# Two of the first loads of an attention and MLP kernel move to another queue, constants go first, and three dummy matmuls are added

## The chip, the cores and the metric

The kernel runs as one program on one core of a Trainium2 chip. The core has five engines with their own instruction streams: TensorE (PE in the rows, with PEld for its weight loads), VectorE (DVE), ScalarE (ACT), GpSimd (POOL) and SyncE (SP). They wait for each other by semaphores. Transfers between main memory and the on-chip buffers are issued by an engine, here almost always SP, and carried out by 16 DMA engines. The metric is the device time of the whole program in microseconds (us); lower is better. The runs shown are medians of three, and one further execution was recorded by the hardware profiler.

## What is computed

The reference takes q, k, v of shape (2, 8, 768, 64), batch, heads, sequence and head size, and runs three stages one after the other:

```python
# 1. linear attention with a decay per head
for t in range(S):
    state = gamma * state + einsum('bhd,bhe->bhde', k[:, :, t], v[:, :, t])
    y[:, :, t] = scale * einsum('bhd,bhde->bhe', q[:, :, t], state)
x = y.transpose(0, 2, 1, 3).reshape(B, S, H * D)            # (2, 768, 512)
# 2. channel mixing with the token before
xk = mu_k * x + (1 - mu_k) * x_prev;  xr = mu_r * x + (1 - mu_r) * x_prev
x = sigmoid(xr @ w_r) * (maximum(xk @ w_k, 0) ** 2 @ w_v)
# 3. gated MLP with a mixing over the sequence
u, v = split(gelu(x @ w_in));  v_n = normalise(v) * g_ln
out = x + (u * (w_sg @ v_n + b_sg)) @ w_out
```

The first stage is the one that the change touches. Of the weights and of q, k and v all bytes come from main memory; the weights arrive as 64-bit floats and are turned into pairs of 32-bit numbers on ACT and DVE.

## The kernel before

The attention is done in chunks of 128 steps, 6 chunks of the sequence times 2 batches, so 12 chunks that are numbered 0 to 11 with the batch changing fastest. Chunk i has two loads of 512 KB each: `qk` (q and k with the feature along the partitions) and `kv` (k and v with the step along the partitions), both issued by `loads` (line 353). For each chunk PE computes

- the scores, key by query, 8 matmuls for the 8 heads (`scores`, line 412, tile `sc`, rows with L416); DVE multiplies them by a mask (`decay`, line 420, tile `prs`, L425),
- the state that the chunk adds, from the keys and the scaled values (`state`, L452, tile `st`); the scaled values `vs` are made on DVE for chunks 0 and 1 (L434) and on POOL for the rest (L430),
- the output from the state of the chunks before (`inter`, L478, tile `y`), which needs a copy of `st` into `scr` that ACT or DVE makes (L249), for all but chunks 0 and 1,
- the output within the chunk (`intra`, L489, tile `y`), from `prs` and `vs`.

In the trace each of these matmuls shows as two, so a chunk's scores are x16. DVE then writes the tokens into `x` (L503), and prepares operands `mix` and `xo` for the second stage, whose matmuls (L327, `kp`, `rp`, `vp`) follow without a break, while the eight pieces of `w_k` are loaded (L256) and converted (L275 to L298).

Before the first scores PE runs ten dummy matmuls of 512 columns on a tile of zeros (`warm_mm`, line 393). `const` (line 363) loads a small table with the mask and the decays, `scratch` (line 374) a table for the outputs.

The order of the instructions on every engine is not written out: each piece of work is handed to a `Plan` (line 54) with an engine, a cost in us, what it reads and writes and the buffers that it takes, and `Plan.order` (line 88) replays these costs and sets the order, and with "DVE ACT" also the engine. Loads go through a model of the transfers there: an issue keeps SP for `ISSUE`, data follow `DMA_LEAD` later at `DMA_RATE`, all in one line (`link`). So a change of a cost or of a queue can move work of all engines. When the program runs, the engines wait only for what they need: data, buffers, and one of eight slots for transfers from the hardware queues, which are used in turn.

Of the kernel before, what the change touches and what calls it, by code (L numbers as in the profile page):

```python
# [33 lines left out]
RSQRT_SEED = float(0x5F3759DF)  # L34
PIECE = 512
WARM_UP = 10
EARLY = 5
CHUNKS = 8
XO = 4
# [8 lines left out]
ISSUE = 0.4  # L48
ADD_ISSUE = 1.2
DMA_LEAD = 1.4  # L50
DMA_TAIL = 2.0
DMA_RATE = 0.41
# [6 lines left out]
class Plan:  # L59
# [28 lines left out]
    def order(self):  # L88
        ops, n = self.ops, len(self.ops)
        left = [len(o[3]) for o in ops]  # L90
        after = [[] for _ in ops]
# [10 lines left out]
                wait.setdefault(pool, []).append((i, kind))  # L102
        home = {}
        pending = {}
        engines = ("PE", "DVE", "ACT", "POOL", "SP", "ADD")
        idle = {e: BEGIN for e in engines}
        queue = {e: [] for e in engines}
        seq, events, link = [], [(BEGIN, -1, e) for e in engines], 0.0
        started = [False] * n

        def put(i):
# [26 lines left out]
            return True  # L138

        def start(i, t, eng):  # L140
            nonlocal link
            engs, cost, fn, deps, new = ops[i]
            engs = engs.split()
            if len(engs) > 1:
                cost = cost[engs.index(eng)]
            for e in engs:
                queue[e].remove(i)
            on[i] = eng
            started[i] = True
            for pool, kind, buf, make in new:  # L150
                free[pool] -= 1
                held[pool, kind] = held.get((pool, kind), 0) + 1
                home[buf] = (pool, kind)
                wait[pool].remove((i, kind))
            if eng in ("SP", "ADD"):
                busy = t + (ISSUE if eng == "SP" else ADD_ISSUE)
                late = link > t + DMA_LEAD + 1.0
                link = max(t + DMA_LEAD, link) + cost / DMA_RATE
                done = link + (DMA_TAIL if late else 0.8)
            else:  # L160
                busy = done = t + cost
            idle[eng] = busy
            seq.append(i)
            heapq.heappush(events, (done, i, "near"))
            heapq.heappush(events, (done + LINK, i, "far"))
            heapq.heappush(events, (busy, n, eng))
# [5 lines left out]
        while events:  # L172
            t = events[0][0]
            while events and events[0][0] <= t + 1e-9:
                _, i, eng = heapq.heappop(events)
# [29 lines left out]
def fused_kernel(ctx, tc, qk, kv, w_k, w_v, w_r, w_in, w_sg, w_out, consts, ydec, b_sg, out):  # L205
# [32 lines left out]
    def new_b(kind, buf):  # L238
        return new("ps", kind, buf, (128, 512))
# [113 lines left out]
    def loads(i, what):  # L353
        b, c = chunks[i]
        hold = [(("kv", 0), 0)] if i > 1 else []
        if "q" in what:
            plan.op("SP", .525, lambda: sp.dma_start(out=T["qk", i], in_=qk[b, c]), r=hold, w=[(("qk", i), 0)],
                    new=[new_p("chunk", ("qk", i), (128, 2, KD, CH), F32)])
        if "v" in what:
            plan.op("SP", .525, lambda: sp.dma_start(out=T["kv", i], in_=kv[b, c]), r=hold, w=[(("kv", i), 0)],  # L360
                    new=[new_p("chunk", ("kv", i), (128, 2, H, D), F32)])

    def const():
# [25 lines left out]
        w = T["warm"] = pools["t"].tile([128, 512], BF16, tag="t", name="warm")  # L389
        dve.memset(w, 0.0)  # L390

    def warm_mm():
        for _ in range(WARM_UP):
            pe.matmul(out=T["warmps"], lhsT=T["warm"][:, :128], rhs=T["warm"], start=True, stop=True)

    prs_new = ("bA", "prs", "prs", products)
    scr_new = ("bB", "scr", "scr", lambda: None)
    plan.op("DVE", .3, warm, w=[("warm", 0)], new=[("t", "warm", "warm", lambda: None)])
    plan.op("PE", 4.0, warm_mm, r=[("warm", 0)], w=[("warmps", 0)], new=[new_b("warm", "warmps")])
    loads(0, "q")  # L400
    plan.op("SP", .11, const, w=[("con", 0)])
    loads(0, "v")
    loads(1, "qv")
    plan.op("SP", .26, scratch, r=[(("kv", 0), 0)], w=[("scr", "yd")], new=[scr_new])
# [89 lines left out]
    def tokens(c):  # L494
        n, off = divmod(c * CH, BW)
        x = ("x", n)
        if off == 0 and n == 0:
            plan.op("DVE", .1, lambda: dve.memset(T[x][:, :, :, 0:1], 0.0), w=[(x, "p")],
                    new=[new("x", "x", x, (128, KD, B, BW + 1))])
        for e in range(2):  # L500
            def scale(e=e):
                table = T["yt", c % 2] if c else T["yd"]
                dve.tensor_tensor(out=T[x][:, e::2, :, 1 + off:1 + off + CH],  # L503
                                  in0=T["y", c, e].rearrange("p (b j t) -> p j b t", b=B, t=CH),
                                  in1=table[:, e::2].unsqueeze(2).to_broadcast([128, KD // 2, B, CH]), op=ALU.mult)
            plan.op("DVE", .66, scale, r=[(("y", c, e), 0), ("scr", ("yt", c % 2) if c else "yd")], w=[(x, (e, off))],
                    new=[new("x", "x", x, (128, KD, B, BW + 1))] if off == 0 and e == 0 and n else [])
        if off == 0 and n:
            plan.op("DVE", .15, lambda: dve.tensor_copy(T[x][:, :, :, 0:1], T["x", n - 1][:, :, :, BW:BW + 1]),
                    r=[(("x", n - 1), (e, CH)) for e in range(2)], w=[(x, "p")])  # L510

    for c in range(NCH):
        pair = (B * c, B * c + 1)
        for i in pair:
            if i > 1:
                loads(i, "qv")
        for step in (scores, decay, inter, state, intra):
            for i in pair:
                step(i)
        tokens(c)  # L520

    def prep(n, kk, i):
# [492 lines left out]
```

## Time and profile before

| | us |
|---|---|
| median of 3 runs (lowest, highest) | 357.09 (356.94, 358.16) |
| the profiled execution | 359.38 |
| its span, from first to last instruction | 357.60 |
| PE busy in it | 347.6 (97%) |
| DVE, ACT, POOL busy | 255.8 (72%), 159.7 (45%), 28.8 (8%) |
| granted TensorE clock, mean | 1.00 |

The span is shorter than the execution's own time by 1.78 us that lie around it. PE's share is so high that the few stretches in which it is not busy are where the time is decided, and these lie in the first 45 us and in the last 12. Over the first 40 us the transfers fill the 16 DMA engines: in the page's 40 slices of 8.9 us the first four carry 252, 415, 408 and 409 GB/s, later ones rarely over 200. The constants are 106 KB, the output table 256 KB, every chunk load and every piece of `w_k` 512 KB.

A row of the timeline gives start and length of a group of equal instructions, then engine, line, operation, tiles and count, and in brackets how long the engine stood idle before it and what ended that.

### The profile page before, as it was taken

How to read it: one execution, taken by the hardware profiler on the slowest of the kernel's cores; microseconds unless marked ns; L12 is line 12 of the kernel's file. 1: busy time of each engine (PE TensorE's matmuls, PEld its weight loads, DVE VectorE, ACT ScalarE, POOL GpSimd, SP SyncE). 2: the span in 40 equal slices, each digit the busy share in tenths (PEclk: the TensorE clock that was granted, in tenths of full speed). 3: DMA queues.
4: the chain of work that ended last, by engine and by line, in shares of the span. 5: the costliest groups of instructions: out<-in, count | busy, mean ns of one | idle time of the engine just before them, and what ended most of it. 6: DMA issues, size and time to landing. Idle time of an engine off the chain costs nothing.

```text
span 357.6 us, 5412 instructions
## 1 busy us (share of the span) xinstructions
PE 347.6 (97%) x2130; PEld 289.7 (81%) x2130; DVE 255.8 (72%) x501; ACT 159.7 (45%) x274; POOL 28.8 (8%) x29
## 2 busy tenths in 40 slices
PE   7988999999999999999999999999999999999995
PEld 4777788888888888888888888888888888899884
DVE  1778999898992664568699998999995656535431
ACT  1044669888972543345589659734542000000000
POOL 0453400000002122101100000000000000000000
PEclk9999999999999999999999999999999999999999
DMA  7999555135544669406354245121130000110122
GB/s 252 415 408 409 210 185 170 59 92 161 158 141 98 106 183 168 73 3 173 66 172 119 60 122 173 44 79 55 45 88 2 0 0 0 60 59 2 58 90 89
DMA packets 15689, 43.32 MB, mean 121 GB/s; under 512 B 1456, under 2 KB 3632, under 8 KB 15664
## 3 DMA queue, kind: packets, MB, share of 16 engines
q1 hardware_dynamic: 12944, 37.73, 30.9%
q0 software_dynamic: 2720, 5.24, 8.6%
q8 instruction: 17, 0.28, 0.3%
q14 instruction: 8, 0.07, 0.1%
HBM read 32.48 MB, written 3.15 MB: 100 GB/s over the span
## 4 chain that ended last, share of the span: by engine, by line
PE 88%; DMA 7%; DVE 3%; issue 1%; SPq 0%; ACT 0%; DVEq 0%; ACTq 0%
PE vp L327 26%; PE kp L327 18%; PE sp L327 14%; PE up L327 9%; PE rp L327 9%; PE op L327 7%; DMA chunk<-qk 3%; DMA chunk<-kv 2%; DMA out<-o 2%; PE y L489 2%; PE sc L416 1%; PE y L478 1%; DVE o L910 1%; DVE xo L316 1%; PE st L452 1%
## 5 line engine op out<-in xcount | busy, mean ns | idle before, releaser
L327 PE MATMUL kp<-xo,wk 128*128 128x512 f32 x288 | 66.2, 390 | 0.0
L327 PEld LDWEIGHTS kp<-xo,wk 128*128 128x128 f32 x288 | 53.9, 188 | 11.5 <-issue 0.3
L327 PE MATMUL sp<-wsg,vh 128*128 128x512 f32 (+1 forms) x288 | 50.2, 336 | 0.0
L327 PEld LDWEIGHTS sp<-wsg,vh 128*128 128x128 f32 x288 | 44.4, 190 | 5.7
L327 PE MATMUL vp<-k,wv 128*128 128x512 f32 x168 | 38.9, 389 | 0.0
L327 PEld LDWEIGHTS vp<-k,wv 128*128 128x128 f32 x168 | 31.5, 188 | 6.5
L327 PE MATMUL vp<-win,x2o 128*128 128x512 f32 x144 | 33.3, 389 | 0.0
L327 PE MATMUL up<-x2o,win 128*128 128x512 f32 x144 | 33.1, 389 | 0.0
L327 PE MATMUL rp<-xo,wr 128*128 128x512 f32 x144 | 33.1, 389 | 0.0
L327 PE MATMUL op<-gt,wout 128*128 128x512 f32 x144 | 33.0, 389 | 0.0
L327 PEld LDWEIGHTS rp<-xo,wr 128*128 128x128 f32 x144 | 27.0, 188 | 5.6
L327 PEld LDWEIGHTS vp<-win,x2o 128*128 128x128 f32 x144 | 27.0, 188 | 5.6
L327 PEld LDWEIGHTS up<-x2o,win 128*128 128x128 f32 x144 | 27.0, 188 | 5.6
L327 PEld LDWEIGHTS op<-gt,wout 128*128 128x128 f32 x144 | 27.0, 188 | 5.6
L888 DVE SCALAR_TENSOR_TENSOR g<-sp,con,bsg 128x512 f32<-128x512 f32 x12 | 9.0, 751 | 21.8 <-PE sp L327 21.8
L316 DVE TENSOR_TENSOR xo<-mix,xo 128x512 fp32r<-128x512 f32 x24 | 17.0, 735 | 8.9 <-ACT xo L249 8.8
L910 DVE TENSOR_TENSOR o<-op,x 128x256 f32<-128x256 f32 (+1 forms) x20 | 8.8, 474 | 19.8 <-PE op L327 13.8
L275 ACT ACTIVATE cv<-raw 128x512 f32<-128x512 f32 x32 | 21.5, 670 | 1.9 <-DMA raw<-w_in 0.7
L327 PE MATMUL vp<-k,ws 128*128 128x512 f32 x96 | 22.1, 389 | 0.0
L612 POOL DMA_DIRECT2D raw<-wv x10 | 12.1, 1211 | 116.9 <-DMA raw<-wv 86.4
L327 PEld LDWEIGHTS vp<-k,ws 128*128 128x128 f32 x96 | 18.0, 188 | 3.7
L290 DVE SCALAR_TENSOR_TENSOR cv<-cv,raw 128x512 int32<-128x512 int32 x28 | 19.8, 714 | 0.6 <-ACT raw L283 0.6
(104 smaller groups left out, 464.5 us busy)
## 6 DMA issues: line engine op xcount, KB each, us to landing
chunk<-qk SPq DMA_DIRECT2D x12, 512.0 KB, 10.1
chunk<-kv SPq DMA_DIRECT2D x12, 512.0 KB, 10.1
raw<-wv POOLq DMA_DIRECT2D x10, 512.0 KB, 5.1
raw<-w_k SPq DMA_DIRECT2D x8, 512.0 KB, 5.3
raw<-w_v SPq DMA_DIRECT2D x8, 512.0 KB, 3.6
raw<-w_in SPq DMA_DIRECT2D x8, 512.0 KB, 3.5
out<-o SPq DMA_DIRECT2D x12, 256.0 KB, 2.2
raw<-w_sg SPq DMA_DIRECT2D x6, 384.0 KB, 3.2
```

Of the source, the lines that this page charges most:

```text
L275: plan.op("ACT", .68, lambda: act.activation(out=xf(), in_=word(1).bitcast(F32), func=ACTF.Prelu, scale=-F64_REBIAS * F64_SIGN, alpha=1.0 ...
L290: dve.scalar_tensor_tensor(out=xi(), in0=xi(), scalar=3, in1=word(0), op0=ALU.logical_shift_left, op1=ALU.bitwise_or)
L316: plan.op("DVE", .69, lambda: dve.tensor_tensor(out=lo(), in0=src(), in1=hi(), op=ALU.subtract), r=[*keep, (buf, ("hi", part))], w=[(buf, ...
L327: pe.matmul(out=T[ps][:, cols], lhsT=l(), rhs=r(), start=first and q == 0 and i == 0, stop=q == 2 and i == len(grp) - 1, skip_group_check= ...
L416: pe.matmul(out=T["sc", i, p][:, j * CH:(j + 1) * CH], lhsT=a[par[p], 1, j], rhs=a[par[p], 0, j], start=j == 0, stop=j == KD - 1, skip_gro ...
L452: pe.matmul(out=st[par[p], b, j], lhsT=T["kv", i][:, 0, h], rhs=T["vs", i][:, h], start=c == 0 and b == 0 and j == 0, stop=b == B - 1 and ...
L478: pe.matmul(out=y_at(i, j, p), lhsT=T["sbd", (c - 1) % 2][par[p], b, j], rhs=T["qk", i][par[p], 0, j], start=b == 0 and j < 2, stop=False, ...
L489: pe.matmul(out=y_at(i, j, p), lhsT=T["vs", i][:, 2 * j + p], rhs=T["pr", i % 4][:, p, j], start=c == 0 and b == 0 and j < 2, stop=b == B ...
L612: plan.op("ADD", .53, lambda t=t: pool.dma_start(out=T[raw], in_=block_view(*t), accum_op=ALU.add), r=[(b, ("hi" if not t[2] else "lo", p) ...
L888: dve.scalar_tensor_tensor(out=out_, in0=in_, scalar=T["vec"][:, 2, m:m + 1], in1=t.unsqueeze(1).to_broadcast([128, B, BW]) if last else t ...
L910: plan.op("DVE", .69 if g == B else .42, lambda n=n, ps=ps, o=o, m=m, part=part, of=of: dve.tensor_tensor(out=T[o][:, part], in0=T[ps][:, ...
```

## The change

The loads of `kv` for chunks 0 and 1 are issued by ACT instead of SP. The constants are issued before the first chunk. Three dummy matmuls are put behind the scores of chunk 0. In the planner's model ACT gets a line of transfers of its own ("AQ"), which runs at half rate, as does SP's until 7.5 us; the ten dummies cost 4.3 instead of 4.0.

```diff
--- before.py
+++ after.py
@@ -34,6 +34,8 @@
 RSQRT_SEED = float(0x5F3759DF)
 PIECE = 512
 WARM_UP = 10
+FILL = 3
+SHARED = 7.5
 EARLY = 5
 CHUNKS = 8
 XO = 4
@@ -102,10 +104,11 @@
                 wait.setdefault(pool, []).append((i, kind))
         home = {}
         pending = {}
-        engines = ("PE", "DVE", "ACT", "POOL", "SP", "ADD")
+        engines = ("PE", "DVE", "ACT", "POOL", "SP", "ADD", "AQ")
         idle = {e: BEGIN for e in engines}
         queue = {e: [] for e in engines}
         seq, events, link = [], [(BEGIN, -1, e) for e in engines], 0.0
+        link2 = 0.0
         started = [False] * n
 
         def put(i):
@@ -138,7 +141,7 @@
             return True
 
         def start(i, t, eng):
-            nonlocal link
+            nonlocal link, link2
             engs, cost, fn, deps, new = ops[i]
             engs = engs.split()
             if len(engs) > 1:
@@ -152,11 +155,15 @@
                 held[pool, kind] = held.get((pool, kind), 0) + 1
                 home[buf] = (pool, kind)
                 wait[pool].remove((i, kind))
-            if eng in ("SP", "ADD"):
-                busy = t + (ISSUE if eng == "SP" else ADD_ISSUE)
-                late = link > t + DMA_LEAD + 1.0
-                link = max(t + DMA_LEAD, link) + cost / DMA_RATE
-                done = link + (DMA_TAIL if late else 0.8)
+            if eng in ("SP", "ADD", "AQ"):
+                busy = t + (ADD_ISSUE if eng == "ADD" else ISSUE)
+                if eng == "AQ":
+                    link2 = max(t + DMA_LEAD, link2) + 2 * cost / DMA_RATE
+                    done = link2 + 0.8
+                else:
+                    late = link > t + DMA_LEAD + 1.0 and t > SHARED
+                    link = max(t + DMA_LEAD, link) + (2 if link < SHARED else 1) * cost / DMA_RATE
+                    done = link + (DMA_TAIL if late else 0.8)
             else:
                 busy = done = t + cost
             idle[eng] = busy
@@ -357,7 +364,7 @@
             plan.op("SP", .525, lambda: sp.dma_start(out=T["qk", i], in_=qk[b, c]), r=hold, w=[(("qk", i), 0)],
                     new=[new_p("chunk", ("qk", i), (128, 2, KD, CH), F32)])
         if "v" in what:
-            plan.op("SP", .525, lambda: sp.dma_start(out=T["kv", i], in_=kv[b, c]), r=hold, w=[(("kv", i), 0)],
+            plan.op("SP" if hold else "AQ", .525, lambda: (sp if hold else act).dma_start(out=T["kv", i], in_=kv[b, c]), r=hold, w=[(("kv", i), 0)],
                     new=[new_p("chunk", ("kv", i), (128, 2, H, D), F32)])
 
     def const():
@@ -389,16 +396,16 @@
         w = T["warm"] = pools["t"].tile([128, 512], BF16, tag="t", name="warm")
         dve.memset(w, 0.0)
 
-    def warm_mm():
-        for _ in range(WARM_UP):
+    def warm_mm(count):
+        for _ in range(count):
             pe.matmul(out=T["warmps"], lhsT=T["warm"][:, :128], rhs=T["warm"], start=True, stop=True)
 
     prs_new = ("bA", "prs", "prs", products)
     scr_new = ("bB", "scr", "scr", lambda: None)
     plan.op("DVE", .3, warm, w=[("warm", 0)], new=[("t", "warm", "warm", lambda: None)])
-    plan.op("PE", 4.0, warm_mm, r=[("warm", 0)], w=[("warmps", 0)], new=[new_b("warm", "warmps")])
+    plan.op("PE", 4.3, lambda: warm_mm(WARM_UP), r=[("warm", 0)], w=[("warmps", 0)], new=[new_b("warm", "warmps")])
+    plan.op("SP", .11, const, w=[("con", 0)])
     loads(0, "q")
-    plan.op("SP", .11, const, w=[("con", 0)])
     loads(0, "v")
     loads(1, "qv")
     plan.op("SP", .26, scratch, r=[(("kv", 0), 0)], w=[("scr", "yd")], new=[scr_new])
@@ -517,6 +524,9 @@
         for step in (scores, decay, inter, state, intra):
             for i in pair:
                 step(i)
+                if step is scores and i == 0:
+                    plan.op("PE", .65, lambda: warm_mm(FILL), r=[("warm", 0)], w=[("warmps", 0)],
+                            after=plan.writer[("sc", 0, 0), 0])
         tokens(c)
 
     def prep(n, kk, i):
```

What the planner makes of it, at three places. First the loads at the start of SP's stream; chunk_93, 110, 112, 114, 133 are qk 0, kv 0, qk 1, kv 1, qk 2, and scr0 takes the output table. Before:

```order
L357 DMA chunk_93<-qk 128x1024
L372 DMA con_108<-consts 128x212
L360 DMA chunk_110<-kv 128x1024
L357 DMA chunk_112<-qk 128x1024
L360 DMA chunk_114<-kv 128x1024
L381 DMA scr0_128<-ydec 128x512
L357 DMA chunk_133<-qk 128x1024
```

Now, with chunk_108, 112, 133 for qk 0, 1, 2 and chunk_135 for kv 2:

```order
L379 DMA con_93<-consts 128x212
L364 DMA chunk_108<-qk 128x1024
L364 DMA chunk_112<-qk 128x1024
L388 DMA scr0_120<-ydec 128x512
L364 DMA chunk_133<-qk 128x1024
L367 DMA chunk_135<-kv 128x1024
```

and at the start of ACT's stream, where the two loads stand ahead of the table that ACT loads for its functions (chunk_110 and 114 are kv 0 and kv 1):

```order
L1020 UNCONDITIONAL_BRANCH
L367 DMA chunk_110<-kv 128x1024
L367 DMA chunk_114<-kv 128x1024
L256 ACT_TABLE_LOAD
L256 COPY scr0_120<-st_147 128x512
```

The constants moved from second to first, and the two `kv` loads from SP, where they stood third and fifth, to ACT, where nothing stands ahead of them.

Second the start of PE's stream, from the last of the ten dummies on, to the first output from the state (L478, now L485). Before:

```order
L394 MATMUL warm<-warm 128x512
L416 MATMUL sc<-chunk 128x128 x8
L452 MATMUL st<-vs,chunk 64x64 x8
L489 MATMUL y<-prs_137,vs 64x128 x8
L416 MATMUL sc<-chunk 128x128 x16
L452 MATMUL st<-vs,chunk 64x64 x8
L489 MATMUL y<-prs_137,vs 64x128 x8
L478 MATMUL y<-chunk,scr_128 64x128 x8
```

Now (two of the three dummies left out):

```order
L401 MATMUL warm<-warm 128x512
L423 MATMUL sc<-chunk 128x128 x8
...
L401 LDWEIGHTS warm
L401 MATMUL warm<-warm 128x512
L459 MATMUL st<-vs,chunk 64x64 x8
L496 MATMUL y<-prs_142,vs 64x128 x8
L423 MATMUL sc<-chunk 128x128 x8
L459 MATMUL st<-vs,chunk 64x64 x8
L423 MATMUL sc<-chunk 128x128 x8
L496 MATMUL y<-prs_142,vs 64x128 x8
L485 MATMUL y<-chunk,scr_120 64x128 x8
```

Beside the dummies, the state of chunk 1 now comes before the scores of chunk 2, and the output of chunk 1 after them.

Third, PE from the state of chunk 2 to the output of chunk 5. Before:

```order
L452 MATMUL st<-vs,chunk 64x64 x8
L489 MATMUL y<-prs_138,vs 64x128 x8
L452 MATMUL st<-vs,chunk 64x64 x8
L489 MATMUL y<-prs_138,vs 64x128 x8
L416 MATMUL sc<-chunk 128x128 x16
L478 MATMUL y<-chunk,scr_129 64x128 x16
L452 MATMUL st<-vs,chunk 64x64 x8
L489 MATMUL y<-prs_137,vs 64x128 x8
L452 MATMUL st<-vs,chunk 64x64 x8
L489 MATMUL y<-prs_137,vs 64x128 x8
```

Now:

```order
L459 MATMUL st<-vs,chunk 64x64 x8
L496 MATMUL y<-prs_143,vs 64x128 x8
L423 MATMUL sc<-chunk 128x128 x8
L459 MATMUL st<-vs,chunk 64x64 x8
L496 MATMUL y<-prs_143,vs 64x128 x8
L485 MATMUL y<-chunk,scr_121 64x128 x8
L423 MATMUL sc<-chunk 128x128 x8
L485 MATMUL y<-chunk,scr_121 64x128 x8
L459 MATMUL st<-vs,chunk 64x64 x8
L496 MATMUL y<-prs_142,vs 64x128 x8
L459 MATMUL st<-vs,chunk 64x64 x8
L496 MATMUL y<-prs_142,vs 64x128 x8
```

The scores of chunk 4 moved ahead of the state and output of chunk 3, and those of chunk 5 behind the first output of chunk 4. Further on the scores of chunk 8 stand directly ahead of chunk 8's output from the state, where before a state and an output of chunk 7 stood between. On SP two pieces of `w_k` moved ahead of the `qk` of chunk 7, and one behind its `kv`. From the first full run of second-stage matmuls on, PE's stream is the same as before.

## Rows read from the trace of the kernel before

**Rows 1.** Stretches: busy time of each engine, then clock, DMA share, GB/s.
```profile
core 0: us, PE busy (x) PEld busy (x) DVE busy (x) ACT busy (x) POOL busy (x), PEclk, DMA share, GB/s
0.00:4.00 4.00, 2.81 (x7) 1.04 (x8) 0.29 (x2) 1.28 (x1) 0.20 (x4) 1.00 0.54 174
4.00:6.50 2.50, 2.50 (x12) 1.23 (x12) 0.17 (x1) 0.00 (x0) 0.00 (x0) 1.00 0.85 224
6.50:8.00 1.50, 1.01 (x12) 0.82 (x9) 0.33 (x1) 0.00 (x0) 0.00 (x0) 1.00 1.03 412
34.00:38.00 4.00, 2.93 (x56) 2.20 (x54) 4.00 (x6) 1.62 (x3) 2.17 (x2) 1.00 1.03 412
45.30:345.40 300.10, 300.10 (x1417) 251.40 (x1414) 221.61 (x448) 142.86 (x248) 12.11 (x10) 1.00 0.33 90
```

**Rows 2.** Chain of waits that ended last: start, length, what.
```profile
10.22 11.15 DMA chunk<-qk
...
25.66 1.91 issue
...
45.41 1.12 PE kp L327 x4
...
48.55 34.72 PE kp L327 x152
```

**Rows 3.** Timeline of PE, from the start to 35 us.
```profile
1.20 4.45 PE L394 MATMUL warm<-warm 128*128 128x512 bf16 x10 [1.20 <-DVE x L498]
5.57 1.94 PE L416 MATMUL sc<-chunk 64*128 64x128 f32 x16
8.42 0.69 PE L452 MATMUL st<-vs,chunk 128*64 128x64 f32 x16 [0.91 <-DVE vs L434]
...
10.63 1.16 PE L416 MATMUL sc<-chunk 64*128 64x128 f32 x16
...
14.87 0.67 PE L478 MATMUL y<-chunk,scr 64*64 64x128 f32 x16
...
18.54 0.63 PE L452 MATMUL st<-vs,chunk 128*64 128x64 f32 x16
...
21.51 1.16 PE L416 MATMUL sc<-chunk 64*128 64x128 f32 x16 [0.19 <-DMA chunk<-qk]
...
34.50 0.38 PE L416 MATMUL sc<-chunk 64*128 64x128 f32 x2 [0.24 <-issue]
```

**Rows 4.** Timeline of DVE, the first 11 us.
```profile
4.34 0.17 DVE L407 TENSOR_SCALAR omu<-con 128x8 f32<-128x8 f32 x1 [3.18 <-DMA con<-consts]
7.67 0.69 DVE L434 TENSOR_TENSOR vs<-chunk,con 128x512 f32<-128x512 f32 x1 [3.16 <-DMA chunk<-kv]
...
10.23 0.69 DVE L434 TENSOR_TENSOR vs<-chunk,con 128x512 f32<-128x512 f32 x1 [0.67 <-DMA chunk<-kv]
```

**Rows 5.** Timeline of SP's issues (SPq), early and later.
```profile
4.37 0.88 SPq L360 DMA_DIRECT2D chunk<-kv  x1
...
22.67 0.33 SPq L357 DMA_DIRECT2D chunk<-qk  x1
23.95 0.33 SPq L360 DMA_DIRECT2D chunk<-kv  x1
```

**Rows 6.** Timeline of POOL: scaling of chunk 4's values.
```profile
20.17 1.04 POOL L430 TENSOR_TENSOR vs<-chunk,con 128x512 f32<-128x512 f32 x1 [3.08 <-DMA chunk<-kv]
```

**Rows 7.** DMA queues from 24.9 to 26.3 us: packets, MB, share.
```profile
q8 instruction: 1, 0.02, 4.8%
```

**Rows 8.** Timeline of all engines, 34 to 38 us.
```profile
34.43 1.52 DVE L533 SCALAR_TENSOR_TENSOR mix<-x,con,mix 128x512 f32<-128x512 f32 x1
...
36.57 0.58 ACT L249 COPY scr<-st 128x512 f32<-128x512 f32 x1
...
37.20 0.67 PE L478 MATMUL y<-chunk,scr 64*64 64x128 f32 x16 [0.83 <-ACT scr L249]
```

**Rows 9.** Timeline of DVE: last low half of the first weight.
```profile
61.47 0.68 DVE L298 TENSOR_TENSOR wk<-cv,wk 128x512 fp32r<-128x512 f32 x1
```

## The prediction

> **What bounds the kernel now.** First the stretches: between 45.30 and 345.40 us TensorE (PE) is busy 300.10 of 300.10 us, and the 357.6 - 345.4 = 12.2 us after that belong to the last results and their stores [rows 1]. The matmuls there are the same ones before and after the change, in the same order, so 312 of the 357.6 us can only stay or get worse. What the change can win lies ahead of 45.3 us, in the attention stage.
>
> Second the chain of waits for that part: it is DMA until 21.37, then PE, with a hole of 1.91 us at 25.66 that nothing in the program explains [rows 2]. Third, PE's timeline and the queues beside it, for the start, where the change is.
>
> I call chunk i's loads qk i and kv i, its score, state and two output products sc i, st i, y i and, with the earlier state, x i. PE runs ten dummies from 1.20 to 5.65 at 0.43 us each, sc0 from 5.57 with no wait before it, st0 at 8.42 after a wait of 0.91 for DVE, y0, and sc1 at 10.63 [rows 3]. 512 columns in 0.43 us are the pace of 1.2 GHz; sc0 runs at it too (1.94 us against 1.16 for sc1), although the stretches print a granted clock of 1.00. VectorE (DVE) has the constants at 4.34, kv0 only at 7.67, kv1 at 10.23 [rows 4]. So the start is held by kv0, third in the queue, and not by qk0.
>
> **The start, step by step.** The same eight transfers are issued, six on SyncE (SP) and two on ScalarE (ACT). Nobody waits for an issue, and ACT, which issues two of them now, has nothing to do from 4 to 8 us [rows 1]. What delays landing is the engines that move bytes: 224 GB/s from 4.0 to 6.5 us, 412 after it [rows 1]. In the weak stretch 2.5 x (412-224)/412 = 1.14 us of transfer were lost, just when an issue took 0.88 us, where it takes 0.33 later [rows 5]. Rows do not say why. In the forecast it happens again.
>
> Constants, qk0 and kv0 are 0.106 + 0.524 + 0.524 = 1.154 MB. In the old order qk0 came first; now it shares its time with kv0, and both are in when all 1.154 MB are. By the stretches 4.0 x 174 GB/s = 0.69 MB had moved by 4.0 and the rest, 0.46 at 224 GB/s, by 6.1. Constants and first chunk (0.63 MB) had moved before 4.0 and were seen at 4.34, so I add 0.4: both are there at 6.5. Bounds: 5.6 (qk0 in its old place, no wait) and 7.7 (kv0's old place). The Trainium skill (DMA: Bandwidth & Descriptors, Issuing engines are not separate DMA queues) says the same against this change: DMAs from SP, ACT and POOL run on the same 16 engines and interleave, and a second issuer saves issue time alone. No run here shows two such queues yet; by this rule the second queue brings no byte earlier, and the working does without it.
>
> So sc0 starts at 6.5 instead of 5.57 and, at the pace of 1.94 us, ends at 8.4. The three dummies behind it cost 3 x 0.43 = 1.3 us at the low clock, half of it at the high one; no row shows which, so I take the middle, 0.95: to 9.35. Behind them wait st0 and everything else on PE. Part of that is covered, as y0 has to wait for DVE's first masking pass, about 0.7 us after sc0. st0 takes 0.6, to 9.95; kv0's scaling (0.69) is long done, which saves the wait of 0.91 before st0 [rows 3]; y0 1.05, to 11.0. qk1 and kv1 close the same sum of bytes as kv1 did, 10.23 [rows 4]. Then sc1 to 12.1, st1 (0.5) to 12.6, sc2 to 13.7 (now ahead of y1), y1 to 14.6. Before: 14.87 [rows 3]. The start gains 0.3 us, between 0.6 gained and none with the dummies' two prices.
>
> **Where that goes.** From y1 both orders do x2, sc3, x3, st2, y2: from 14.87 to 18.54 then [rows 3], 3.7 us, so now to 18.3. The new order then puts sc4 ahead of st3 and y3. kv4 lands at 20.17 [rows 6], and issues that wait for a free slot come 1.28 us apart, one load each [rows 5], so qk4 lands about 18.9: PE waits 0.6. Then sc4 1.1, st3 0.5, y3 0.9, x4 0.5, sc5 1.1 and x5 0.5 end at 23.6. Before, sc5 waited for qk5 until 21.51 [rows 3] and with it x4 and x5 were through 2.1 us later, at 23.6. So 0: the loads, whose sum and start do not change, take back whatever the start wins, and a start up to 0.6 us later than worked out here costs nothing either.
>
> The hole from 25.66 to 27.57 stands ahead of y5 and has no releaser, only "issue" [rows 2]. In the 1.4 us around it the DMA rows show one transfer of the instruction queue, 0.02 MB [rows 7]; PE seems to have run out of instructions while their fetch stood behind data. The Trainium skill (Runtime: NRT & Kernel Launch, Instruction fetch mechanics) has PE refilled in 16 KiB blocks, the cost of a boundary "mostly hidden". The trace agrees on the block and not on the hiding: 1.91 us here. By the rule the hole would be something else; the sum carries it unchanged either way. Six more PE instructions move the boundary by six. I leave the hole as it is: 0. Bounds: down to the next such hole, 0.24 at 34.50 [rows 3], so -1.7; and as much again, +1.9.
>
> **34 to 38 us.** PE is busy 2.93 of 4.00 us [rows 1]. 0.83 of the rest is x8 waiting for ACT's copy of the state, which came at 36.57, behind a cast that itself waited for a DVE pass of 1.52 us (other passes over as many elements take 0.69 [rows 4]) [rows 8]. The new order has sc8 (1.09) between y7 and x8, so PE has work while the copy is made: -0.8. Bounds 0 (the wait turns up elsewhere) and -1.07.
>
> **Weight loads, later stages.** On SP two w_k pieces are now ahead of qk7: +2 x 1.28 = 2.56 us for it. It stood five loads behind kv4 (20.17 [rows 6]), so at 26.6, and goes to 29.1; y5 ends 1.0 after the hole, at 28.6, and sc7 comes at 28.6 + 1.1 + 0.5 + 0.5 = 30.7, a cover of 1.6 us. If the hole went, some 0.3 would show. DVE and ACT share the weight conversions in another way; the last w_k piece is through at 62.2 [rows 9] and wanted by the eighth result of 12 matmuls each, of which four came at 45.41: at 48.55 + (84-4) x 34.72/152 = 66.8 [rows 2], 4.6 us of slack. In the long stretch DVE is busy 74% and ACT 48% [rows 1]: 0, at worst some tenths.
>
> **Sum.** Start and loads 0, hole 0, state copy -0.8, rest 0: -0.8. On the profiled execution 359.38 - 0.8 = 358.6. The median before is 357.09, 2.29 under that execution, so I forecast 357.09 - 0.8 = **356.3 us**.
>
> **Rivals.**
> - *The weak stretch of the transfers goes.* It coincides with slow issues in one queue, which speaks for it; that bytes first moved well with the same queue speaks against. Then every load is 1.1 us earlier, sc0 starts at 5.6, PE reaches the hole about 1.0 earlier, and if the fetch is asked for earlier too, all of it lasts: -1.0 - 0.8 = -1.8, 355.3. With the hole shrunk as well, 354.
> - *PE goes idle after the dummies and stays slow (slower).* sc0 waits for qk0 until 7.7: 2.1 us of idle PE at the low clock, sc0 to 9.65, dummies 1.3 to 10.95, st0 and y0 to 12.6, sc1, st1, sc2, y1 to 16.3: 1.4 later than before. The loads hide 0.3 of it up to the hole, but the hole's end is pushed by the full 1.4 if the fetch is asked for at PE's pace; and the state copy is then asked for at another moment, so its gain is not sure: +1.4, 358.5, or 357.7 with that gain. It decides from sc0 later than about 7. For it speaks kv0's row at 7.67, against it that 0.69 MB had moved by 4.0.
> - *Nothing is left.* The start washes out as worked above, and DVE's and POOL's collisions fall on another state copy: 357.1.
>
> **How the numbers follow.** Forecast 0.40, weak stretch gone 0.24, slow start 0.13, nothing left 0.23. 0.5% of 357.09 is 1.8 us, about what a measurement of this kernel tells from no change: under 355.3 is faster, over 358.9 slower. Half of the second case and some tenths of a shrunken hole in the first give 0.22 faster; slow starts with a grown hole give 0.09 slower; 0.69 between. The range holds the forecast with the bounds of hole and copy, most of the weak-stretch case (down to 354.6) and the slow start (358.4).
>
> **What would show it.** Right: sc0 at 6 to 7 with a gap behind the dummies, kv0 seen on DVE beside it, kv1 at about 10.2, sc4 waiting for a DMA near 18.9, a hole without releaser near y5, no ACT wait ahead of x8, and PE without idle time from about 44.5. Wrong: 400 GB/s between 4 and 6.5 us and sc5 before 20.5 (the first rival); sc0 after 7, or sc1 still at 1.9 us (the second); PE waiting for anything after 46 us, which the sum puts at nothing.

## The result, and the profile after

The changed kernel takes 359.53 us (median of 9 runs, 358.30 to 360.33) against 356.93 (9 runs, 356.69 to 358.16) of the kernel before on the same chip: ratio 1.0066, 95% interval 1.0048 to 1.0084. It is slower on this chip, above the forecast of 356.3 and above the range. Its profiled execution took 359.12 us with a span of 356.9.

The stretches after, to be laid beside [rows 1]: busy time and number of instructions of each engine, then granted clock, DMA share and GB/s.

```profile
core 0: us, PE busy (x) PEld busy (x) DVE busy (x) ACT busy (x) POOL busy (x), PEclk, DMA share, GB/s
0.00:4.00 4.00, 2.81 (x7) 1.04 (x8) 0.29 (x2) 1.28 (x1) 0.20 (x4) 1.00 0.49 126
4.00:6.50 2.50, 1.01 (x4) 0.24 (x2) 0.86 (x2) 0.00 (x0) 0.00 (x0) 1.00 1.03 421
...
8.00:12.00 4.00, 4.00 (x45) 2.67 (x44) 2.39 (x3) 0.00 (x0) 2.04 (x2) 0.62 1.03 410
...
34.00:38.00 4.00, 4.00 (x74) 3.24 (x70) 4.00 (x8) 2.99 (x5) 1.11 (x2) 1.00 1.02 402
...
45.30:345.40 300.10, 300.04 (x1413) 251.22 (x1413) 221.22 (x448) 143.90 (x248) 12.14 (x10) 1.00 0.33 90
```

One of the forecast's two signs of the first rival stands in them: between 4.0 and 6.5 us the transfers move 421 GB/s instead of 224, so the weak stretch is gone (in the 4 us ahead of it they move less, 126 instead of 174). The other sign, sc 5 before 20.5, failed: it starts at 23.23. PE is busy for only 1.01 of the 2.5 us, and from 8 to 12 us it has a granted clock of 0.62, which fits the second rival. The stretch 34 to 38 us is full, 4.00 of 4.00, where it was 2.93.

PE's timeline after, for [rows 3]: start, length, operation, in brackets the idle time ahead and what ended it.

```profile
1.19 3.81 PE L401 MATMUL warm<-warm 128*128 128x512 bf16 x10 [1.19 <-DVE x L505]
7.55 2.03 PE L423 MATMUL sc<-chunk 64*128 64x128 f32 x16 [2.55 <-DMA chunk<-qk]
9.52 1.46 PE L401 MATMUL warm<-warm 128*128 128x512 bf16 x3
10.91 0.73 PE L459 MATMUL st<-vs,chunk 128*64 128x64 f32 x16
...
12.45 1.16 PE L423 MATMUL sc<-chunk 64*128 64x128 f32 x16
...
23.23 1.16 PE L423 MATMUL sc<-chunk 64*128 64x128 f32 x16
...
44.01 1.20 PE L334 MATMUL kp<-xo,wk 128*128 128x512 f32 x4
45.14 2.73 PE L496 MATMUL y<-prs,vs 128*64 128x128 f32 x32
```

PE waits 2.55 us for qk 0, then runs sc 0 and the dummies at half its pace; st 0 starts at 10.91 instead of 8.42. So the second rival's sign "sc0 after 7" came; its other one, sc 1 at 1.9 us, did not (1.16 at 12.45). PE never waits for a load or an engine again before the long stretch. The result products of chunks 10 and 11 (y at 45.14) take 2.73 us, against 1.97 in the trace of the kernel before that follows below. DVE, for [rows 4]: the constants at 4.82, and kv 0, for which it waited until 7.67 before, at 5.14, with nobody to use it until sc 0 is done. The last two lines show why y 10 and y 11 are slow: three conversions take DVE 3.39 us (1.88 in the kernel with qk 0 first, below), and so it makes the `prs` that these products read only from 44.25 to 46.72.

```profile
4.82 0.17 DVE L414 TENSOR_SCALAR omu<-con 128x8 f32<-128x8 f32 x1 [3.67 <-DMA con<-consts]
5.14 0.69 DVE L441 TENSOR_TENSOR vs<-chunk,con 128x512 f32<-128x512 f32 x1
9.61 1.29 DVE L432 TENSOR_TENSOR prs<-sc,con 128x512 f32<-128x512 f32 x2 [3.78 <-PE sc L423]
...
39.66 3.39 DVE L297 SCALAR_TENSOR_TENSOR cv<-cv,raw 128x512 int32<-128x512 int32 x3
...
44.25 2.47 DVE L432 TENSOR_TENSOR prs<-sc,con 128x512 f32<-128x512 f32 x4
```

Why qk 0 came so late stands in the DMA queues of the changed kernel from 3 to 4 us (q10 is ACT's queue, q1 SP's; packets, MB, share of the 16 engines):

```profile
q10 hardware_dynamic: 82, 0.34, 81.5%
q1 hardware_dynamic: 77, 0.06, 18.2%
```

The two queues got nearly the same number of packets through, but SP's were those of the constants, 0.8 KB each, and ACT's those of kv 0, 4.1 KB each. While the constants stand in front of qk 0, ACT's queue takes the bytes. The Trainium skill (DMA: Bandwidth & Descriptors, Queues, rings and completion order) says that each DMA engine goes round between the queues it has work for, a packet at a time; the 82 to 77 packets agree, as far as a packet of these rows is what the page calls one. The counts are not always that close: in the kernel with qk 0 first (below) the constants pass from 4 to 5 us, and there SP's queue has 112 packets and 0.13 MB, ACT's 69 and 0.22 MB. In both stretches the queue with the small packets moves fewer bytes.

### The profile page after: what moved, and what is told of

Its sections match the earlier page's. It is cut to its first block, busy times and chain, and to the rows that moved or that the text cites. A ratio compares the mean times of both kernels' runs of the same rounds, so it can differ in the third digit from the quotient of the medians.

```text
span 356.9 us, 5411 instructions
## 1 busy us (share of the span) xinstructions
PE 348.9 (98%) x2133; PEld 289.9 (81%) x2133; DVE 256.1 (72%) x501; ACT 160.2 (45%) x274; POOL 28.8 (8%) x29
## 3 DMA queue, kind: packets, MB, share of 16 engines
q10 hardware_dynamic: 288, 1.05, 0.7%
## 4 chain that ended last, share of the span: by engine, by line
PE 83%; DMA 11%; DVE 4%; SPq 0%; issue 0%
PE vp L334 26%; PE kp L334 18%; PE sp L334 14%; PE up L334 9%; PE rp L334 9%; DMA chunk<-qk 7%; PE op L334 7%; DMA chunk<-kv 2%; DMA out<-o 2%; DVE prs L432 1%; DVE cv L297 1%; DVE o L920 1%; DVE x L510 1%; PE y L496 0%; DVE xo L323 0%
## 5 line engine op out<-in xcount | busy, mean ns | idle before, releaser
L432 DVE TENSOR_TENSOR prs<-sc,con 128x512 f32<-128x512 f32 x24 | 15.3, 681 | 7.7 <-PE sc L423 7.6
```

The source lines that it names most:

```text
L432: plan.op("DVE", .66, lambda p=p: dve.tensor_tensor(out=T["pr", i % 4][:, p], in0=heads(T["sc", i, p]), in1=T["mask"].unsqueeze(1).to_broa ...
```

## The experiments

Twelve runs were made, in four groups, each group on one chip beside the kernel before (358.04, 357.77, 357.75 and 358.58 us there). In the expectations, W says that PE's wait for qk 0 and the low clock are what costs, O that the new order does, H that the recorded execution of before was not its usual one, S that recording itself costs; further letters are explained in the expectation in which they first stand. Times are medians. Ratios are to the kernel before in the same group, with 95% intervals; they are not the quotients of the medians. Different groups ran on different chips, so medians are compared within a group. Five numbers of the profiled runs carry most of the reading: when sc 0, st 0 and the first four matmuls of the second stage (kp) start, how long y 10 and y 11 take, and the span, in us.

| profiled run | sc 0 | st 0 | kp x4 | y 10, 11 | span |
|---|---|---|---|---|---|
| before, again | 5.57 | 8.54 | 43.20 | 1.97 | 355.4 |
| changed, again | 7.07 | 10.47 | 43.87 | 2.73 | 356.7 |
| changed, no dummies behind sc 0 | 7.24 | 9.24 | 43.62 | 2.75 | 356.5 |
| new order, loads on SP | 5.04 | 8.66 | 43.05 | 2.72 | 355.9 |
| old order, kv 0 and 1 on ACT | 5.57 | 7.06 | 41.78 | 1.97 | 353.9 |
| the same, 15 dummies | 6.04 | 7.26 | 43.56 | 1.97 | 355.7 |
| changed, 18 dummies | 7.04 | 8.88 | 42.79 | 2.72 | 355.7 |
| the same, POOL writes only | 7.31 | 9.15 | 41.84 | 1.97 | 354.0 |
| changed, qk 0 before constants | 5.57 | 7.67 | 41.20 | 1.97 | 353.3 |
| the same, again | 5.15 | 7.24 | 41.04 | 1.97 | 353.2 |
| the same, no dummies behind sc 0 | 5.26 | 7.41 | 41.52 | 1.97 | 353.7 |
| constants first, qk 0 and kv 0 on ACT | 5.57 | 8.44 | 41.55 | 1.97 | 353.7 |

**The kernel before, unedited.**

> The kernel before, unchanged, recorded once more. Theory H (the recorded execution of before was not a usual one: its hole of 1.91 us ahead of y5, and its own time of 359.38 against a median of 356.93, belong together): the hole is shorter by 1.5 us or more in the new record, or stands elsewhere, and the first second-stage matmul starts at 43 to 43.8 us, not 45.34. Rival S (the record is a usual one and recording itself costs the 2.4 us): hole and 45.3 us come back within 0.3 us. The ratio is 1.000 within 0.2% by both.

357.56 us (356.39 to 359.86, 12 runs), ratio 0.9987 (0.9962 to 1.0011). Its profiled run shows no wait of PE for "issue": the hole of 1.91 us [rows 2] is not in it, nor in any later profiled run of this study. H holds for that term: the trace that the prediction rests on was one of the longer executions.

```profile
12.44 1.16 PE L416 MATMUL sc<-chunk 64*128 64x128 f32 x16 [0.53 <-DMA chunk<-qk]
...
31.80 1.16 PE L416 MATMUL sc<-chunk 64*128 64x128 f32 x16 [0.91 <-DMA chunk<-qk]
...
44.35 1.97 PE L489 MATMUL y<-prs,vs 128*64 128x128 f32 x32
```

It waits for loads, 0.53 and 0.91 us; in these two places they hold the old order.

**The changed kernel without its three dummies.**

```diff
-plan.op("PE", .65, lambda: warm_mm(FILL), ...
+plan.op("PE", .65, lambda: warm_mm(0), ...
```

> The changed kernel with its order and queues, without the three dummies behind chunk 0's scores. Theory W (PE waits for qk0 until 7.5 us, runs at the low clock until about 11, and never idles again, so whatever the start loses stays): the dummies' 1.46 us at the low clock come off in part, since the first masking pass then ends at 10.9 and holds y0: y0 at 10.9 instead of 11.5, total 0.5 to 1.5 us below the changed kernel (358.0 to 359.0). If the dummies are what brings the clock back, chunk 0's outputs run at the low pace instead and nothing is gained or 1 us lost (359.5 to 360.5). Theory O (the order of the work is what costs): no change, 359.5.

358.56 us (12 runs), ratio 0.9992 (0.9970 to 1.0013); two runs at 355.88 and 356.09 with a mean granted clock of 1.0, ten from 357.89 to 358.83 at 0.994 to 0.998. In the profiled run sc 0 still waits (to 7.24) and still takes 2.08 us; st 0 is then slow too (1.12 us). So the dummies behind sc 0 cause neither the wait nor the low pace. What they cost in time is not shown: the changed kernel did not run in this group, and the ratio shows no loss against the kernel before. The median lies in W's range and not at O's 359.5, but these came from times on another chip.

**New order and dummies, the first loads on SP as before.**

```diff
-lambda: (sp if hold else act).dma_start(out=T["kv", i], ...
+lambda: sp.dma_start(out=T["kv", i], ...
+# first five issues put back: qk0, con, kv0, qk1, kv1
```

> The changed kernel's order of work and its dummies, but the first five loads all from SP and in the sequence of before (first chunk's qk, constants, kv, qk, kv). Theory W: chunk 0's scores start at 5.6 again with no idle time behind the ten dummies, so most of the loss goes: 356.5 to 357.5, at or within 0.2% of before. Theory O: the loss stays, 359 to 360.

357.31 us, ratio 0.9966 (0.9941 to 0.9992): no loss against the kernel before. In the profiled run sc 0 starts at 5.04, and the granted clock is 1.00 up to 12 us. O falls; W stands.

**Old order, only kv 0 and kv 1 on ACT.**

```diff
-lambda: sp.dma_start(out=T["kv", i], ...
+lambda: (sp if hold else act).dma_start(out=T["kv", i], ...
```

> The kernel before, in its own order and without the extra dummies, with the kv loads of chunks 0 and 1 issued by ACT and nothing else; qk0 is first on SP. Theory W: qk0 shares with kv0 and lands about 7.0 (constants no longer ahead of it, so 0.3 before the changed kernel), the scores start at 7.0 to 7.3 at the low clock: 1 to 2 us over before, 358 to 359. Theory O: as before, 357.0, or 0.5 to 1 us faster, since the loads behind gain (400 GB/s and over from 4 to 6.5 us).

357.36 us, ratio 0.9956 (0.9934 to 0.9978), in two groups, five runs at 355.78 to 356.16 and seven at 357.3 to 357.8, six of these with a mean clock of 0.995 to 0.997. Here qk 0 is first on SP and is in by 5.57. W had expected it at 7.0 and a loss of 1 to 2 us, because it shares the engines with kv 0; that failed, and the gain of 0.7 us is within what O had named. So a second queue is no loss by itself; with qk 0 in front it is a gain.

**The changed kernel, unedited, on another chip.**

> The changed kernel unedited, beside the next three on one chip. Theory Q (the constants, issued first on SP, push the issue of qk 0 from 0.74 to 1.19 us, behind kv 0 and kv 1 that ACT's queue issues at 0.74; qk 0 then lands near 7.5, PE idles 2.5 us and runs on at half the clock until 11) and theory C (what costs is the idle of PE and the low clock after it, whatever made qk 0 late) both expect it slower than before by 0.4 to 0.9% again, near 359, with clock records under 1.0 in the first 12 us. Theory R (the loss was a matter of that chip and hour, and the start is hidden behind DVE and the loads) expects it level with before within 0.3%.

358.93 us (356.05 to 359.36, 12 runs), ratio 1.0014 (0.9990 to 1.0038). The trace repeats the late start, but three runs of 356.05 to 357.75 blur the ratio; by the ratio alone this group does not tell slower from same, and R is not ruled out by it. The mean clock does not set these three apart (0.999 and 1.0): the slowest run, 359.36, has 1.0 too.

```profile
1.19 4.45 PE L401 MATMUL warm<-warm 128*128 128x512 bf16 x10 [1.19 <-DVE x L505]
7.07 2.08 PE L423 MATMUL sc<-chunk 64*128 64x128 f32 x16 [1.43 <-DMA chunk<-qk]
```

The clock records under 1.0 that Q and C expected in the first 12 us are not there. The ten dummies took 4.45 us, 0.43 us each, which is the pace of 1.2 GHz by the prediction's working, and sc 0 went on at it behind the wait. So here the clock did not fall: PE had not left the lower level when it began to wait, and the profile prints 1.00 all the same. In the first trace the ten dummies took 3.81 us; there PE had left it, and the clock fell behind the wait. The run without the dummies behind sc 0 is like this one (4.45, then 1.59 idle).

**qk 0 ahead of the constants.** The one edit that the rest turns on: order and dummies as changed, kv 0 and kv 1 still on ACT.

```diff
+# first two SP issues swapped: qk0, con
```

> The changed kernel with one pair of issues changed back on SP: qk 0 first, constants second; kv 0 and kv 1 stay on ACT's queue, order and dummies as changed. Theory Q: qk 0 is in before 5.6 as in the run with the order of before and ACT's loads, sc 0 starts by 5.6, no clock record under 1.0 in the profile, st 0 near 7.3 instead of 10.9, kp near 42 to 42.5 instead of 44.0; 356.0 to 357.0, some 2 us under the changed kernel beside it. Theory C alone, with qk 0 late because ACT's queue is served first whatever SP's order: sc 0 still at 7, 358.5 to 359.5. Theory R: within 0.5 us of the changed kernel.

355.38 us (355.31 to 355.71, 6 runs), ratio 0.9933 (0.9909 to 0.9957): faster than both kernels, below Q's range, and with the narrowest spread of all. It is 3.55 us under the changed kernel beside it, so R falls, and C alone with it. Its queues from 3 to 4 us and its PE:

```profile
q1 hardware_dynamic: 49, 0.20, 51.2%
q10 hardware_dynamic: 49, 0.20, 48.8%
```

```profile
5.57 1.41 PE L428 MATMUL sc<-chunk 64*128 64x128 f32 x16
6.91 0.82 PE L405 MATMUL warm<-warm 128*128 128x512 bf16 x3
7.67 0.69 PE L464 MATMUL st<-vs,chunk 128*64 128x64 f32 x16
```

Now qk 0 and kv 0 do share evenly, as the forecast had assumed for the changed kernel; Q holds.

**The changed kernel with 18 first dummies.**

```diff
-plan.op("PE", 4.3, lambda: warm_mm(WARM_UP), ...
+plan.op("PE", 4.3, lambda: warm_mm(18), ...
```

> The changed kernel with 18 dummy matmuls ahead of sc 0 instead of 10 (some 0.21 us each once the clock is up, so that they end at 6.7 to 7.3 instead of 5.0 to 5.6); loads, order and the three dummies behind sc 0 as changed. qk 0 still lands at 7.5. Theory C: sc 0 at 7.5 now takes 1.2 us instead of 2.0 and the three dummies 0.65 instead of 1.46, so st 0 starts near 9.3 instead of 10.9: 1.4 to 1.6 us under the changed kernel beside it, 357.2 to 357.8, with no clock record under 1.0 in the first 12 us. Theory Q with the clock as a mere companion (the lateness of qk 0 is all): no more than 0.4 under the changed kernel. Theory R: the same as the changed kernel within 0.3.

357.36 us (355.79 to 358.28), ratio 0.9978 (0.9957 to 0.9998), 1.6 us under the changed kernel beside it.

```profile
7.04 1.16 PE L423 MATMUL sc<-chunk 64*128 64x128 f32 x16 [0.45 <-DMA chunk<-qk]
8.13 0.82 PE L401 MATMUL warm<-warm 128*128 128x512 bf16 x3
```

qk 0 comes as late as ever (7.04), but PE is idle for 0.45 us instead of 1.43 and sc 0 takes 1.16 instead of 2.08: st 0 is 1.59 earlier (8.88 for 10.47). C holds too: of the late start 1.59 us is the low pace of sc 0 and the dummies (0.92 and 0.64), and from 8.88 to the 7.67 with qk 0 first, 1.21 us, the wait itself. Two groups of times remain.

**Old order, ACT's loads, 15 dummies.**

```diff
-for _ in range(WARM_UP):
+for _ in range(15):
```

> The kernel before with kv 0 and kv 1 issued by ACT, as in the earlier run at 357.36 with two groups of times (355.8 to 356.2 and 357.3 to 357.8), and 15 dummy matmuls ahead of sc 0 instead of 10. If the upper group is the executions in which PE idled before qk 0 and then ran at half the clock (theory C), the dummies cover that wait and nearly all runs lie at 355.8 to 356.4. If the upper group comes from elsewhere (rival: instruction supply or another landing order of the loads), both groups stay, some 1.6 us apart. If the dummies only delay sc 0 and the loads do not bound behind it (theory R), 0.5 to 1.1 us later than the lower group: 356.5 to 357.

356.49 us, ratio 0.9961 (0.9944 to 0.9978); eleven runs at 356.02 to 356.71, one at 357.57, which is the profiled one, at a mean clock of 0.995. C's range holds four of the twelve runs; seven lie up to 0.3 above it, which the later sc 0 (6.04 for 5.57, theory R) would give too. The theory looked at the wrong wait: in the profiled run the start is clean, and the low pace comes behind the wait for qk 8.

```profile
31.27 1.81 PE L416 MATMUL sc<-chunk 64*128 64x128 f32 x16 [1.96 <-DMA chunk<-qk]
33.01 1.12 PE L452 MATMUL st<-vs,chunk 128*64 128x64 f32 x16
33.91 1.58 PE L489 MATMUL y<-prs,vs 128*64 128x128 f32 x16
```

Against 1.16, 0.69 and 1.05 elsewhere that is 1.6 us, the distance of the two groups in the run with 10 dummies, of whose upper group there is no trace. In its profiled run, of the lower group, a like wait of 2.08 us ended without a fall of the clock. Why more dummies at the start make the fall rarer stays open.

**Constants first, qk 0 and kv 0 on ACT, qk 1 and kv 1 on SP.**

```diff
-sp.dma_start(out=T["qk", i], ...
+(act if i == 0 else sp).dma_start(out=T["qk", i], ...
-(sp if hold else act).dma_start(out=T["kv", i], ...
+(act if i == 0 else sp).dma_start(out=T["kv", i], ...
+# first issues in the order con, qk0, kv0, qk1, kv1
```

> The changed kernel with the queues of the first loads dealt otherwise: constants first on SP as changed, qk 0 and then kv 0 on ACT's queue, qk 1 and kv 1 on SP behind the constants; order and dummies as changed. In the changed kernel's trace SP's queue carried 77 packets with 0.06 MB between 3 and 4 us, while ACT's carried 82 with 0.34 MB. Theory Q, sharpened: the constants' small packets hold the queue that they stand in, so what is behind them starts late, and the other queue's first load has the engines almost to itself. Then qk 0 is in near 4.8, sc 0 starts at 5.1 to 5.6 with no idle of PE, kv 0 comes at 7.1 to 7.6 and st 0 starts near 8.3; no clock record under 1.0; 355.4 to 356.4, over 2 us under the changed kernel. Rival (a load that PE needs at once is late whenever the constants go first, on either queue): sc 0 after 6.5 and 357.5 to 359.

The trace is as Q says: sc 0 at 5.57 without a wait, kv 0 at 7.70, st 0 at 8.44, no granted clock under 1.0 up to 12 us. The median, 357.42 (ratio 0.9981, 0.9960 to 1.0001), misses its range: five runs at 355.83 to 356.39 are in it, seven at 357.1 to 358.0 are not. The two groups of the 18 dummies again, and the mean clock does not part them (0.997 to 1.0 in both).

**qk 0 first, without the three dummies; and with them once more.**

> The changed kernel with qk 0 issued ahead of the constants on SP, and without the three dummies behind sc 0. In the run with the dummies sc 0 ended at 6.9, the dummies at 7.67 and st 0 followed at once, while the values it needs were ready near 7.0. Theory F (they only take PE's time there): st 0 at 7.05 to 7.2 instead of 7.67, and 0.3 to 0.6 us less, 354.8 to 355.1, as PE bounds what follows. Theory G (they bridge a wait, and without them PE drops to half the clock): a clock record under 1.0 before 12 us in some executions, and a second group of times 1 to 2 us higher. Theory N (the loads or DVE bound behind the start): 355.2 to 355.6, no difference.

> The changed kernel with qk 0 issued ahead of the constants on SP, once more, as the measure for the two others and to see whether its narrow spread (355.31 to 355.71) holds on another chip. Theory Q expects 355.2 to 355.9 with at most one run in six over 357; a rival by which its six runs were luck among the two groups of the other kernels expects half of the runs near 357 to 359.

355.63 us (355.21 to 355.96) without, 355.46 (355.31 to 355.72) with; ratios 0.9937 (0.9914 to 0.9960) and 0.9937 (0.9914 to 0.9959). N: the dummies neither help nor cost there, since st 0 waits for kv 0's scaling either way (0.99 us without them, 0.18 with), and PE later waits for loads.

**POOL writes only.** From a trace with a time of each group, though of two kernels: in the upper one (18 dummies) DVE's passes with two inputs in SBUF (the large on-chip buffer; PSUM is the one that takes PE's results) are long where POOL's product of kv stands beside them; in the lower one (qk 0 on ACT) POOL is long.

```profile
28.94 1.54 DVE L323 TENSOR_TENSOR xo<-mix,xo 128x512 fp32r<-128x512 f32 x1
...
32.80 1.53 DVE L543 SCALAR_TENSOR_TENSOR mix<-x,con,mix 128x512 f32<-128x512 f32 x1
```

```profile
28.89 1.04 POOL L437 TENSOR_TENSOR vs<-chunk,con 128x512 f32<-128x512 f32 x1
```

That is DVE's timeline with 18 dummies, and POOL's. With qk 0 on ACT, DVE's and then POOL's:

```profile
28.82 0.68 DVE L323 TENSOR_TENSOR xo<-mix,xo 128x512 fp32r<-128x512 f32 x1
...
31.86 0.74 DVE L548 SCALAR_TENSOR_TENSOR mix<-x,con,mix 128x512 f32<-128x512 f32 x1
```

```profile
28.78 1.63 POOL L442 TENSOR_TENSOR vs<-chunk,con 128x512 f32<-128x512 f32 x1
```

PE stands at the same place (sc 7) at 28.19 and 28.27 in these two runs, and their spans end 2.0 us apart.

```diff
-pool.tensor_tensor(out=T[vs], in0=T["kv", i][:, 1], in1=T["vd"]..., op=ALU.mult)
+pool.memset(T[vs], 0.0)
```

> The changed kernel with 18 dummies ahead of sc 0, in which POOL no longer multiplies the values of chunks 2 and later by their decay: it fills the scaled values with zeros instead, so it writes the same tile and reads nothing. The kernel with 18 dummies had two groups of times, 355.8 to 356.2 and 357.0 to 358.3. In its profiled run, of the upper group, three kinds of DVE instruction with two inputs in SBUF were stretched where POOL's product ran beside them (xo 1.54 us instead of 0.68, mix 1.53 instead of 0.74, three cv 3.38 instead of 1.89), and PE stood 2.0 us longer behind them between 31 and 46. Theory P (POOL's reads and those DVE instructions hold each other up, and which of the two is held decides the group): the stretched xo, mix and cv are back at 0.68 to 0.75 us, y 10 and y 11 take 1.97 and not 2.7, and nearly all runs lie at 355.3 to 356.2. Theory L (the groups come from when the first loads land or from instruction supply of PE): both groups stay, some 2 us apart, with a third or more of the runs over 357. Theory D (DVE is simply too slow for the new order): the stretches go and y 10 and y 11 stay at 2.5 or more, 356.5 to 358.

356.34 us (355.87 to 356.69, 6 runs), ratio 0.9943 (0.9922 to 0.9964): one group, where seven of the twelve runs with 18 dummies lay over 357; four of its six runs are 0.1 to 0.5 above the range given. The groups of DVE's instructions, 12 to 48 us, in this run and then in the changed kernel (count, busy time, mean ns):

```profile
L542 DVE SCALAR_TENSOR_TENSOR mix<-x,con,mix 128x512 f32<-128x512 f32 x5 | 3.6, 745 | 0.0
L297 DVE SCALAR_TENSOR_TENSOR cv<-cv,raw 128x512 int32<-128x512 int32 x5 | 3.2, 680 | 0.0
L323 DVE TENSOR_TENSOR xo<-mix,xo 128x512 fp32r<-128x512 f32 x4 | 2.6, 681 | 0.0
```

```profile
L432 DVE TENSOR_TENSOR prs<-sc,con 128x512 f32<-128x512 f32 x22 | 14.0, 681 | 4.0 <-PE sc L423 3.8
...
L323 DVE TENSOR_TENSOR xo<-mix,xo 128x512 fp32r<-128x512 f32 x4 | 4.0, 1016 | 0.0
L297 DVE SCALAR_TENSOR_TENSOR cv<-cv,raw 128x512 int32<-128x512 int32 x3 | 3.4, 1179 | 0.0
L543 DVE SCALAR_TENSOR_TENSOR mix<-x,con,mix 128x512 f32<-128x512 f32 x4 | 3.2, 830 | 0.0
```

P holds; L and D fall (y 10 and y 11 are back at 1.97). One thing beside it: POOL's fill is also shorter (0.52 us) and waits for no load, so that this run takes away its length as well as its reads. That prs, with only one input in SBUF (the other is PSUM's sc), keeps 681 ns in the changed kernel speaks for the reads. The Trainium skill (SBUF — State Buffer, Who interferes with whom) says just that: a DVE instruction with two SBUF inputs contends with a GpSimd instruction that reads SBUF, not with one that only writes. The Trainium skill says there too that the order of issue decides which of the two is held; the records cannot show that, as POOL's start stands 0.04 to 0.05 us ahead of DVE's in both runs, and once DVE was held and once POOL.

## Why the prediction was wrong, step by step

- *"both are there at 6.5 ... So sc0 starts at 6.5"*: this step failed. It counted bytes and let qk 0 and kv 0 share them evenly. Yet from 3 to 4 us the queue with the constants in front moved 0.06 MB while the other moved 0.34, so kv 0 was in at 5.1 and qk 0 at 7.5 (7.07 in the second trace). With qk 0 in front of the constants the even sharing is there, sc 0 starts at 5.57 and the whole loss is gone. The rule that stands beside this step in the prediction, by which a second queue brings no byte earlier, did not hold either: by the stretches 1.56 MB had moved by 6.5 us (4.0 x 126 + 2.5 x 421 GB/s) instead of 1.26.
- *"the loads, ... take back whatever the start wins, and a start up to 0.6 us later than worked out here costs nothing either"*: failed as well. It held the weak stretch of the transfers fixed (224 GB/s; measured 421), so it kept the loads as the bound. They came earlier, PE waited for none after 7.55, and what sc 0 lost stayed lost. The first two rivals came true at once: the one on the transfers, whose gain PE could not use, and the slow start, whose course was nearly met (sc 0 to 9.65 and dummies to 10.95 on record; 9.6 and 10.98 measured) and which had a chance of 0.13; its 358.5 was still 1.0 below the median. "It decides from sc0 later than about 7" was the right point; 6.5, with bounds of 5.6 and 7.7, was not a safe distance from it.
- *State copy, -0.8*: the wait at x 8 [rows 8] is gone, as predicted. But DVE's passes stay long elsewhere, and y 10 and y 11 take 0.76 more: what the third rival says of collisions, in another place. "PE waiting for anything after 46 us, which the sum puts at nothing" was wrong by that.
- *The hole, "I leave the hole as it is: 0"*: it belonged to one execution. It is in neither trace of the changed kernel, nor in that of before again. Working from that one trace took for the kernel's habit what was that execution's. The prediction's reading of it, instructions that came late, gains by the second trace: there the like transfer of the instruction queue starts at 22.8, 0.7 us after x 4 (22.13); in the first it starts at 25.0, 2.4 us after x 4 (22.60), and the hole follows. Why it came late there is open.
- The sum, from the two traces of the second and first group (changed again, before again): st 0 +1.93, from there to kp -1.26 (33.40 for 34.66, waits for loads gone), y 10 and y 11 +0.76: +1.43; the spans differ by 1.3. That is about half of the 2.6 us between the medians on the first chip. Another 0.4 us lies outside the span, which is 2.2 us shorter than the time in both profiled executions of the changed kernel and 1.8 and 1.7 in those of the one before; with qk 0 first it is 2.2 and 2.1, so it is no part of what the late start costs. The rest stays open.

And from the changed kernel to the one with qk 0 first: st 0 -2.80, from there to kp +0.13, y 10 and y 11 -0.76: -3.43; the spans differ by 3.4. The middle stretch holds unlike things: 0.80 us of waits for loads with qk 0 first, DVE's long passes in the changed kernel. So the gain is the start and, with it, collisions of DVE and POOL that did not occur.

## What to carry to other kernels

When a second queue is opened, look at what stands first in each: a load of many small packets ahead of the one that the busiest engine waits for hands the bytes to the other queue. Before a late start is counted as hidden, ask whether the change also removes what hid it. And take a term from a single trace only if a second execution of the same kernel shows it.

## What was not expected of the hardware

- PE's clock after a wait: after 2.55 us of idle time at the start the granted clock fell (0.62 from 8 to 12 us), and after 1.96 us at 29 to 31 us as well (0.79 from 28 to 36 us, old order with 15 dummies); after 0.45, 0.62, 1.50 (before, again), 1.71 (loads on SP) and 2.08 us (old order, ACT's loads) the work behind it ran at full pace. The idle time alone does not order these. Two further waits, 1.43 and 1.59 us, found PE still at the pace of its dummies, 0.43 us each, and sc 0 went on at it, though the profile prints a clock of 1.00.
- DVE and POOL hold each other up by 0.6 to 0.9 us in the instructions shown in the last experiment. That which of them it hits parts executions of one kernel into groups 2.0 us apart, with no sign in the clock, is likely and not shown: without POOL's reads six runs are one group, but the traces of the two groups are of two kernels.
- Bringing kv 0 in over a second queue, beside qk 0, took the transfers between 4 and 6.5 us from 224 GB/s [rows 1], 232 (before, again) and 292 (new order, loads on SP) to between 361 (qk 0 first, no dummies behind sc 0) and 421 (changed). Why one queue was weak there stays open.
